# Regrouping the last six inverse-transform groups of the first batch with GpSimd copies, so that they run in 128x128 tiles in place of 128x64

## The chip, the cores and the metric

The kernel runs on one core of one Trainium2 chip. The metric is device time in microseconds (us), the median of repeated runs. A core has a matrix engine (TensorE, PE in the profile; its weight loads are listed apart as PEld), a vector engine (VectorE, DVE), a scalar engine (ScalarE, ACT), GpSimd (POOL) and a queue engine (SyncE, SP). POOL and SP also issue DMAs. Each engine works through its own instructions in the order in which the program wrote them and waits for others only by semaphores.

## The reference

For each of 8 batches of 3008 rows and 256 channels, a real FFT along the rows is multiplied by a learned filter and transformed back; the 24064 resulting rows then go through two matrix products with a leaky ReLU between them.

```python
X = np.fft.rfft(x, axis=1)                       # x: (8, 3008, 256)
Y = X * (filt_r + 1j * filt_i)[None]             # filters: (1505, 256)
y = np.fft.irfft(Y, n=3008, axis=1).reshape(24064, 256)
h = y @ w_in                                     # (256, 2048)
out = np.maximum(0.01 * h, h) @ w_out            # (2048, 256)
```

## The kernel before

**The transform.** 3008 is split into N1 x N2 = 94 x 32, with n = 32*n1 + n2. Forward stage 1 contracts over n1 and stage 2 over n2; the filter is applied; inverse stage "sa" contracts over the second frequency index, and inverse stage "sb" contracts over the first and gives 94 rows for each n2. Between the stages the layout has to be turned so that the contracted index lies on the partitions. The channels come in two halves, `dt` = 0 and 1, of 128 each. One sb group handles four values of n2 (h = 0 to 7) for one half `dt`.

**Two ways to run it.** Batches 1 to 7 turn the layout by DMA. For them `s1_group`, `s2_group`, `sa_group` and `sb_group` run a group of four small matmuls each (an s1 or sb group is four matmuls of 128x128 weights with some 94 to 96 moving columns). Batch 0 comes first, when nothing else can run, and is written out by hand in the list `FIRST`; it turns the layout with 32x32 block transposes on DVE (steps `t1`, `t2`). The last `t2` writes its result to `big[0]`. Because a transpose step moves pairs of 16-bit values, the 128 channels of one n2 lie in `big[0]` in two interleaved sets of 64, each with a step of four elements (8 bytes). `sb_matmuls` therefore takes each n2 in two matmuls with 128x64 weights, one writing PSUM partitions 0 to 63 and one 64 to 127: eight matmuls for a group of four n2.

`big[0]` holds 8192 elements a partition: `dt` = 0 in its first half and `dt` = 1 in its second. `FIRST` runs all eight groups of `dt` = 0 (`sbp 0 h`) and the groups h = 0 and 1 of `dt` = 1. The other six, h = 2 to 7 of `dt` = 1, are not needed by the first row chunk; `late_sb` runs them later, at the times in `REST`, in the order h = 2, 4, 5, 3, 7, 6. `quad_copy` evicts each from PSUM to `yt`, the rows that the matrix products read. From the fourth row chunk on, `big[0]` is reused for operand sums.

**The row chunks.** 47 chunks of 512 rows go through `moe1` (16 steps with 128x512 moving operand, evicted in pairs by ACT with the leaky ReLU, L531) and then through the second product: plainly for the first three chunks (`plain`, L693), and for the later ones with a Strassen-like scheme of seven products (`products`, L601, with its sums on DVE at L567).

**The order of the work.** Every piece of work is put with `at(time, f)` on a heap, in planned time units of which a chunk has eight, and is emitted in order of that time. This sets only the order in each engine's queue; the engines run as fast as their semaphores allow. The s1 groups of batch 1 are planned at 0.6-unit steps from the start; `x_load(2, ...)` (POOL-issued, 192 KB each) for batch 2 is planned from 9.6 units; the first filter addition on POOL (`y`, L330) follows after 12.6.

**Lines named below.** L269 and L270: matmuls and eviction of an s1 group. L277: DMA transposes of batch 1 on. L315: matmuls of an s2 group, L321 to L327 its filter products on DVE. L330: the addition on POOL. L337 and L339: sa. L351: eviction in `quad_copy`. L362: matmuls of an sb group of batches 1 to 7. L445: `t2`. L453: matmuls of `sb_matmuls`. L207: `x_load`; L474: load of `w_out`. L721: sums of weights on DVE. L726 to L728: DVE copies of the filter to the lower and upper 64 partitions. PSUM tiles are `ph` (two banks each), `pf` and `po_ps`.

Of the kernel before, what the change touches and what calls it, by code (L numbers as in the profile page):

```python
# [11 lines left out]
P = 128  # L12
# [7 lines left out]
N1, N2 = 94, 32  # L20
NC = 24
Q = 32
# [56 lines left out]
def kernel(  # L79
# [9 lines left out]
    nc = tc.nc  # L89
# [24 lines left out]
    REST = (5.339, 14.69, 8.396, 11.015, 24.419, 20.72)  # L114
# [21 lines left out]
    i1_sb = cpool.tile([P, N2, NW], FP16, name="i1_sb")  # L136
# [7 lines left out]
    HALF = Q * D // 2  # L144
    big = [cpool.tile([P, Q * D + (HALF // 2 if i == 2 else 0)], FP16, name=f"big{i}") for i in range(3)]
# [21 lines left out]
    def bank(kind, n, w, hold=0.75):  # L167
        if kind == "ph":
            t = wide[turn[kind] % 2]
            turn[kind] += 1  # L170
        else:
            i = min(range(len(single)), key=lambda i: frees[i])
            t, frees[i] = single[i], max(frees[i], clock["now"]) + hold
        return t[:, : n * w].rearrange("p (n w) -> p n w", n=n)
# [5 lines left out]
    def at(time, f):  # L180
        clock["n"] += 1
        heapq.heappush(work, (time, clock["n"], f))


    issued = set()

    def need(*what):
        for w in what:
            assert w in issued, w
# [155 lines left out]
    def quad_copy(b, h, dt, ps, copy):  # L345

        start, v, a = (b * N + h * QT) % RING, ps.rearrange("p c a -> p a c"), 0
        while a < N1:
            to = (start + 4 * a) % RING
            n = min(N1 - a, (RING - to) // 4)  # L350
            copy(yt[:, dt, ds(to, 4 * n)].rearrange("p (a c) -> p a c", c=4), v[:, ds(a, n)])  # L351
            a += n
# [15 lines left out]
    act, dve = nc.scalar.copy, nc.vector.tensor_copy  # L368
# [78 lines left out]
    def sb_matmuls(ps, dt, h):  # L447
        assert ("i1t",) not in issued
        src = big[0][:].rearrange("p (h n e r t) -> p h n r t e", h=2, n=Q // 2, r=2, t=2)
        for j in range(4):  # L450
            n2 = 4 * h + j
            for t in range(2):
                nc.tensor.matmul(ps[64 * t : 64 * t + 64, j, :], src[:, dt, n2 // 2, n2 % 2, t, :],  # L453
                                 i1_sb[:, n2, :N1], start=True, stop=True)
# [6 lines left out]
    def sbe(dt, h, e):  # L461
        quad_copy(0, h, dt, held.pop(("sb", dt, h)), engine[e])

    def late_sb(dt, h, copy):
        ps = bank("pf", 4, NW)[:, :, :N1]
        sb_matmuls(ps, dt, h)
        quad_copy(0, h, dt, ps, copy)

    def load_x(half):
        x_load(1, half * N2 // 2, N2 // 2)  # L470
# [229 lines left out]
        return [lambda tj=tj, ct=ct: one(tj, ct) for tj in range(4) for ct in range(NCT)]  # L700

    groups, first_use = [], {}
    for g in range(10, 16):
        at(REST[g - 10], lambda g=g: late_sb(1, g - 8, (act, dve)[g < 12 and g % 2]))

    def plan(b, s1, s1_step, s2, s2_step, lag, sb, sb_step, xl, x_step):
        for g in range(16):
# [23 lines left out]
    for b in range(1, B):  # L731
        z = 47 * (b - 4) if b > 4 else 0
        p = PLANS[min(b, 4) - 1]
# [23 lines left out]
    while queue:  # L757
        time, n, stage, b, g, f = heapq.heappop(queue)
        t = max(time, last + GAP)
# [64 lines left out]
```

## Time and profile before

| what | value |
|---|---|
| runs | 742.13 us median of 3 (745.01, 740.62, 742.13) |
| profiled execution | 740.67 us, its span from first to last instruction 738.9 us |
| granted TensorE clock | 0.999 |
| PE busy | 731.1 us (99%), PEld 522.1 us (71%) |
| DVE, ACT, POOL busy | 509.1, 549.1, 167.8 us (69, 74, 23%) |

The profile shows one execution, so a sum over its rows is made against 740.67 us. Busy shares are averages over the whole span; the change concerns the stretch from about 33 to 80 us, and there the timeline of each engine has to be read. A line of the timeline gives start, duration, engine, line of the program, operation, output and input, the number of instructions merged into it, and in brackets the idle time before it with what ended it. The start of the next PE line tells how long a group of matmuls held the stream; the duration in the line includes the drain of the last one.

### The profile page before, as it was taken

The numbers are of one execution on the slowest core, as the hardware profiler recorded it, in microseconds if no ns is written. First come the engines' busy times: TensorE is split into PE (matmuls) and PEld (weight loads), VectorE is DVE, ScalarE is ACT, GpSimd is POOL, SyncE is SP. The second block draws the span as 40 slices with busy tenths as digits, with TensorE's granted clock in tenths as the row PEclk, the third lists the DMA queues.
The fourth block names the chain that finished last, engine by engine and source line by source line (L and its number), as shares of the span: only waits on it lengthen the run. The fifth ranks groups of instructions, "written<-read, shape, count | busy, mean of one in ns | idle before, by whom it ended". The sixth has DMA issues, their size and how long they took to land.

```text
span 738.9 us, 19530 instructions
## 1 busy us (share of the span) xinstructions
PE 731.1 (99%) x8129; PEld 522.1 (71%) x8129; DVE 509.1 (69%) x696; ACT 549.1 (74%) x763; POOL 167.8 (23%) x171
## 2 busy tenths in 40 slices
PE   8999999999999999999999999999999999999997
PEld 3666677777777777777777777777767777777776
DVE  7978557776677667676777667676767686465566
ACT  4775787887788778887688877888767777777762
POOL 5605411433122322212232323122031210000000
PEclk9999999999999999999999999999999999999999
DMA  9978779777855595556855577434853432112012
GB/s 205 229 109 169 189 152 180 163 176 162 193 134 119 142 195 143 130 144 120 190 130 136 124 155 172 115 91 109 151 171 94 120 106 91 58 55 66 29 45 72
DMA packets 128617, 98.44 MB, mean 133 GB/s; under 512 B 59296, under 2 KB 107296, under 8 KB 128336
## 3 DMA queue, kind: packets, MB, share of 16 engines
q1 hardware_dynamic: 112752, 79.30, 41.8%
q0 software_dynamic: 15056, 17.50, 15.6%
q8 instruction: 63, 1.03, 0.6%
q10 hardware_dynamic: 720, 0.39, 0.2%
q14 instruction: 26, 0.21, 0.1%
HBM read 45.97 MB, written 35.65 MB: 110 GB/s over the span
## 4 chain that ended last, share of the span: by engine, by line
PE 95%; DVE 1%; DMA 1%; SPq 1%; ACT 1%; POOL 0%; issue 0%; POOLq 0%; DVEq 0%
PE ph L528 42%; PE pf L601 18%; PE po_ps L601 18%; PE pf L362 2%; PE pf L269 2%; PE pf L337 2%; PE pf L315 2%; PE po_ps L384 2%; PE pf L693 1%; PE po_ps L693 1%; DMA p_b_g<-p_b_g 1%; SPq L277 1%; POOL y_b_g L330 0%; PE pf L436 0%; ACT yt L351 0%; PE ph L412 0%
## 5 line engine op out<-in xcount | busy, mean ns | idle before, releaser
L531 ACT ACTIVATE gt_c<-ph 128x1024 f16<-128x1024 f32 x376 | 385.1, 1024 | 133.1 <-PE ph L528 126.2
L528 PE MATMUL ph<-yt,w_in_sb 128*128 128x512 f16 x1504 | 447.3, 379 | 0.2 <-ACT yt L351 0.2
L601 PEld LDWEIGHTS <-gt_c 128*128 128x128 f16 x2800 | 201.8, 98 | 98.2 <-issue 1.6
L330 POOL TENSOR_TENSOR y_b_g<-p_b_g,p_b_g 128x512 f16<-128x512 f32 x84 | 118.2, 1409 | 422.0 <-DMA p_b_g<-p_b_g 287.0
L601 PEld LDWEIGHTS <-big 128*128 128x128 f16 x2128 | 151.4, 98 | 65.9
L528 PEld LDWEIGHTS <-w_in_sb 128*128 128x128 f16 x1504 | 117.7, 98 | 4.4 <-DVE yt L351 0.4
L324 DVE TENSOR_TENSOR p_b_g<-pf,fb_sb 128x512 f32<-128x512 f32 x78 | 53.7, 689 | 33.4 <-PE pf L315 20.2
L601 PE MATMUL po_ps<-wt_sb,gt_c 128*128 128x128 f16 x704 | 71.8, 219 | 0.0
L601 PE MATMUL pf<-wt_sb,gt_c 128*128 128x128 f16 x688 | 69.3, 219 | 0.0
L601 PE MATMUL pf<-wt_sb,big 128*128 128x128 f16 x704 | 68.7, 219 | 0.0
L601 PE MATMUL pf<-w_out_sb,gt_c 128*128 128x128 f16 x720 | 68.1, 219 | 0.0
L351 ACT CAST yt<-pf 128x376 f16<-128x376 f32 (+9 forms) x136 | 58.2, 441 | 12.2 <-PE pf L362 8.5
L601 PE MATMUL po_ps<-w_out_sb,gt_c 128*128 128x128 f16 x688 | 65.7, 219 | 0.0
L601 PE MATMUL po_ps<-wt_sb,big 128*128 128x128 f16 x688 | 65.5, 219 | 0.0
L567 DVE TENSOR_TENSOR big<-big,gt_c 128x2048 f16<-128x2048 f16 (+1 forms) x45 | 57.5, 1278 | 0.1
L327 DVE TENSOR_TENSOR p_b_g<-pf,fa_sb 128x512 f32<-128x512 f32 x84 | 57.2, 681 | 0.2
L567 DVE TENSOR_TENSOR big<-gt_c 128x2048 f16<-128x2048 f16 (+1 forms) x46 | 56.8, 1234 | 0.0
L567 DVE TENSOR_TENSOR big<-gt_c,big 128x2048 f16<-128x2048 f16 (+1 forms) x45 | 56.6, 1258 | 0.0
L567 DVE TENSOR_TENSOR gt_c<-gt_c 128x2048 f16<-128x2048 f16 x43 | 55.6, 1293 | 1.0
L339 ACT CAST big<-pf 128x512 f16<-128x512 f32 x84 | 49.0, 583 | 9.3 <-PE pf L337 7.4
L270 ACT CAST big<-pf 128x384 f16<-128x384 f32 x90 | 43.0, 479 | 10.9 <-PE pf L269 8.3
L362 PE MATMUL pf<-i_sb,big 128*128 128x94 f16 x448 | 37.0, 206 | 0.0
(98 smaller groups left out, 645.8 us busy)
## 6 DMA issues: line engine op xcount, KB each, us to landing
p_b_g<-p_b_g SPq DMA_DIRECT2D x156, 128.0 KB
out_dram<-ost_c_h SPq DMA_DIRECT2D x117, 128.0 KB
dz<-big SPq DMA_DIRECT2D x42, 256.0 KB
big<-dz SPq DMA_DIRECT2D x56, 192.0 KB
x_sb<-in_x_dram POOLq DMA_DIRECT2D x40, 192.0 KB, 4.2
x_sb<-in_x_dram POOLq DMA_DIRECT2D x2, 768.0 KB, 9.4
w_in_sb<-in_moe_w_in_dram POOLq DMA_DIRECT2D x1, 1024.0 KB, 13.6
w_out_sb<-in_moe_w_out_dram POOLq DMA_DIRECT2D x1, 1024.0 KB, 14.5
```

Source lines behind the costliest of these rows:

```text
L269: nc.tensor.matmul(ps[:, j, :], x_sb[:, 4 * h + j, ts(dt, P)], fwd1m[:, :NW], start=True, stop=True)
L270: copy(turn_in[:, :, dt, :, ds(4 * h, 4)], ps.rearrange("p n (q k) -> p k q n", q=4))
L324: nc.vector.tensor_tensor(p2[:], ps, fb, AL.mult)
L327: nc.vector.tensor_tensor(p1[:], ps, fa, AL.mult)
L330: ("y", b, g), lambda: nc.gpsimd.tensor_tensor(y1[:], p1[:], p3[:], AL.add)))
L339: nc.scalar.copy(st2[h % 3][:, ds(2 * (g % 2), 2), :], ps)
L351: copy(yt[:, dt, ds(to, 4 * n)].rearrange("p (a c) -> p a c", c=4), v[:, ds(a, n)])
L362: nc.tensor.matmul(ps[:, j, :], z2[h % 3][:, j, ts(dt, P)], i1_sb[:, 4 * h + j, :N1], start=True, stop=True)
L528: nc.tensor.matmul(ph[:, j, :], w_in_sb[:, dt, ts(ct, P)], yt[:, dt, ds(ci * CH % RING, CH)], start=(dt == 0), stop=(dt == NDT - 1))
L531: nc.scalar.activation(gts[ci][:, ds(2 * g, 2), :], ph, AF.Lrelu)
L567: nc.vector.tensor_tensor(*(v[:, ds(c0, n)] for v in (o, i0, i1)), op)
L601: nc.tensor.matmul(of[t], a()[:, c, ts(t, P)], w[:, c, :], start=(c == 0), stop=(c == NCH - 1))
```

## The change

Six copies on GpSimd, emitted right after the hand-written list (planned time 0.02, in the order h = 2, 4, 5, 3, 7, 6), read the `dt` = 1 half of `big[0]`, which has the 8-byte step, and write it in plain [n2][channel] order into `rest`, the first 3072 elements of `big[0]`. That place held `dt` = 0, whose groups have run by then. Each copy moves 128 partitions x 512 16-bit elements. `late_sb` then runs each n2 in one matmul with 128x128 weights out of `rest`, four for a group in place of eight. Its planned times, its PSUM banks and its evictions stay.

```diff
+    rest = big[0][:, : 24 * P].rearrange("p (n d) -> p n d", d=P)
+
+    def regroup(h):
+        src = big[0][:, HALF:].rearrange("p (n e x) -> p n x e", n=Q // 2, x=4)
+        nc.gpsimd.tensor_copy(rest[:, ts(h - 2, 4)].rearrange("p (n r) (t e) -> p n (r t) e", r=2, t=2), src[:, ts(h, 2)])
+        issued.add(("rest", h))
+
-    def late_sb(dt, h, copy):
+    def late_sb(h, copy):
         ps = bank("pf", 4, NW)[:, :, :N1]
-        sb_matmuls(ps, dt, h)
-        quad_copy(0, h, dt, ps, copy)
+        need(("rest", h))
+        for j in range(4):
+            nc.tensor.matmul(ps[:, j, :], rest[:, 4 * (h - 2) + j], i1_sb[:, 4 * h + j, :N1], start=True, stop=True)
+        quad_copy(0, h, 1, ps, copy)
...
     groups, first_use = [], {}
+    for h in (2, 4, 5, 3, 7, 6):
+        at(0.02, lambda h=h: regroup(h))
     for g in range(10, 16):
-        at(REST[g - 10], lambda g=g: late_sb(1, g - 8, (act, dve)[g < 12 and g % 2]))
+        at(REST[g - 10], lambda g=g: late_sb(g - 8, (act, dve)[g < 12 and g % 2]))
```

## The prediction

> **What bounds the kernel now.** I read the page first, for the bound:
>
> ```profile
> PE 731.1 (99%) x8129; PEld 522.1 (71%) x8129; DVE 509.1 (69%) x696; ACT 549.1 (74%) x763; POOL 167.8 (23%) x171
> PE 95%; DVE 1%; DMA 1%; SPq 1%; ACT 1%; POOL 0%; issue 0%; POOLq 0%; DVEq 0%
> ```
>
> PE is busy for 731.1 of 738.9 us, and 95% of the chain that ended last is PE. So PE time taken out of the middle should come off the end, unless the stage it is taken from waits for something else. Next, the groups by shape from 0 to 110 us, for the prices (busy us, mean ns):
>
> ```profile
> L453 PEld LDWEIGHTS <-big 128*64 128x64 f16 x128 | 4.6, 154 | 2.6 <-issue 1.6 <-DVE big L445 1.0
> L269 PEld LDWEIGHTS <-x_sb 128*128 128x128 f16 x128 | 8.6, 98 | 4.4
> L330 POOL TENSOR_TENSOR y_b_g<-p_b_g,p_b_g 128x512 f16<-128x512 f32 x12 | 15.1, 1269 | 35.8 <-DVE p_b_g L327 26.6 <-DMA p_b_g<-p_b_g 5.6 <-PE pf L315 2.9
> ```
>
> A 64-column load from the stepped layout takes 154 ns, a plain one of 128 columns 98. Then the PE timeline around the first and the last of the six late groups, where the starts count:
>
> ```profile
> 40.81 0.59 PE L528 MATMUL ph<-yt,w_in_sb 128*128 128x512 f16 x2
> 41.34 0.45 PE L453 MATMUL pf<-i_sb,big 128*64 128x94 f16 x8
> 41.71 0.34 PE L269 MATMUL pf<-small_sb,x_sb 128*128 128x96 f16 x4
> 41.89 1.03 PE L528 MATMUL ph<-yt,w_in_sb 128*128 128x512 f16 x4
> 42.76 0.33 PE L269 MATMUL po_ps<-small_sb,x_sb 128*128 128x96 f16 x4
> ...
> 79.43 0.49 PE L693 MATMUL po_ps<-w_out_sb,gt_c 128*128 128x256 f16 x3
> 79.85 0.45 PE L453 MATMUL pf<-i_sb,big 128*64 128x94 f16 x8
> 80.23 0.60 PE L528 MATMUL ph<-yt,w_in_sb 128*128 128x512 f16 x2
> ```
>
> Last, DVE from 33 to 47 us with the DMA share of two stretches, and one place later on where POOL and DVE meet:
>
> ```profile
> 37.40 0.96 DVE L726 TENSOR_SCALAR fb_sb<-fa_sb 64x3072 f16<-64x3072 f16 x1
> 40.19 0.95 DVE L727 COPY fb_sb<-fa_sb 64x3072 f16<-64x3072 f16 x1
> 42.09 0.56 DVE L270 CAST big<-pf 128x384 f16<-128x384 f32 x1 [0.50 <-PE pf L269]
> 43.62 0.56 DVE L270 CAST big<-po_ps 128x384 f16<-128x384 f32 x1 [0.97 <-ACT gt_c L531]
> 44.21 0.95 DVE L728 COPY fa_sb<-fa_sb 64x3072 f16<-64x3072 f16 x1
> 45.19 1.02 DVE L270 CAST big<-pf 128x384 f16<-128x384 f32 x2
> ```
>
> ```profile
> 40.00:45.00 5.00, 5.00 (x52) 2.95 (x51) 3.50 (x6) 4.76 (x8) 0.00 (x0) 1.00 0.84 136
> 45.00:50.00 5.00, 4.93 (x46) 3.42 (x45) 3.26 (x7) 3.77 (x5) 0.00 (x0) 1.00 0.01 2
> ```
>
> ```profile
> 159.61 1.28 POOL L330 TENSOR_TENSOR y_b_g<-p_b_g,p_b_g 128x512 f16<-128x512 f32 x1 [5.20 <-DVE p_b_g L324]
> 160.03 1.94 DVE L567 TENSOR_TENSOR gt_c<-gt_c 128x2048 f16<-128x2048 f16 x1
> ```
>
> **What is removed: 24 of 48 small matmuls.** Four L528 go from 41.89 to 42.76, so a pair holds the stream 0.43 us; the pair at 40.81 was done at 41.24. The late group starts at 41.34, after a hole of 0.10, and the next work at 41.71: 0.47 us in all. At 79.43 three L693 (0.11 each: four go from 45.23 to 45.67) end at 79.76, and the next L528 starts at 80.23: 0.47 again; the groups at 51.58, 58.69 and 71.77 give the same. The new form, four matmuls with plain 128x128 weights and 94 columns, is almost the L269 group: 41.71 to 41.89, 0.17 to 0.18 us, with no hole ahead. So 0.47 - 0.17 = 0.30 us a group, 1.8 us for six.
>
> [...] Eight 64-column matmuls take 41.34 to 41.71, 46 ns each; four 128-column ones take 43 ns each. The two halves of an n2 do not run side by side. [...]
>
> **What of it reaches the end.** The first two late groups stand where ACT and DVE hold the chain: it runs L528 at 42.06, ACT L531 at 42.53, then DVE L270, L728 and L270 until 46.21, then the L269 at 46.27 that needed a bank. ACT had idled 0.23 us for PE before 42.53, so of the first 0.30 only 0.23 passes on. The group at 45.76 lies ahead of the L269 that waits for DVE, with a hole of 0.13 behind it already: its saving turns into a longer hole, so I count 0. The other four stand in a stream of PE work without such a hole: 4 x 0.30 = 1.2. After 110 us PE waits for another engine only twice, both for L330, 1.3 us in all, and these waits hang on filter products that PE itself released, so they move with it. Sum: 0.23 + 0 + 1.2 = 1.4 us.
>
> **What is added: six copies on POOL.** They need the last `t2` (DVE, ends 33.67) and, for h = 7, the last `dt` = 0 group (PE, before 34.5). The trace has no one-input copy on POOL and none with an 8-byte step. Nearest rows: L330, two 32-bit inputs of the same 512 elements, 1.27 us; L416, one 32-bit and one 16-bit input, 1.16 us mean. One input should be less; bounds 0.6 (half of 1.27) to 2.4 us (the longest L330 in this trace, 2.36, while it met DVE). I take 1.0, near L416. [...]
>
> Six copies and two meetings with DVE (L726, L727, 0.96 each) end at 33.67 + 6.0 + 1.9 = 41.6 us. The first is done by 34.7, needed at 41.34; the second by 35.7, needed at 45.76; the others are needed at 51.58, 58.69, 71.77 and 79.85. PE does not wait unless one copy takes over 6 us. The cover on POOL is its idle time: it issues the `w_out` load at 28.38, two `x_load`s of batch 2 at 36.46 and 37.67, and then nothing until L330 at 57.24. The two loads are queued behind the copies and move to about 41.6 and 42.2, landing by about 49 to 50 (7.4 us from issue). Their rows are first read at 82.08. They leave a full stretch of DMA (share 0.84) for an empty one (0.01), and end about where the first DMA transpose is issued (48.87): no charge. Were the copies 2.4 us each, these loads would run beside the transposes that the L315 at 54.57 waits for.
>
> **What is added on DVE: meetings with POOL.** Evictions from PSUM beside L330 keep their time (L324 and L327 at 57.13 and 57.73, inside an L330, took 0.69 and 0.68). L567, with both inputs in SBUF, took 1.94 instead of 1.22 us at 160.03: the 0.72 extra is about the rest of the L330 that ended at 160.89. The trace shows no L726-like one-input copy beside POOL. Bounds: nothing, or a full copy (1.0) for each of L726 and L727. I take half a copy each, 1.0 us by 41 us, at no cost: DVE idles 0.50 before 42.09 and 0.97 before 43.62, and a PSUM bank comes round only four groups later (the eviction that ends at 38.94 frees the bank used at 40.64). Without that cover up to 0.5 us would pass on.
>
> [...]
>
> **Sum.** 740.67 - 1.4 = 739.3 us for the profiled execution. That one lay 1.46 under the median of the runs; against the median, 742.13 - 1.4 = 740.7 us. Half a per cent, 3.7 us, is about what a measurement of this kernel can tell from no change, so this counts as none.
>
> **Rivals.**
> *The copies are slow, and DVE pays.* If a copy takes c, copies are still running when L728 starts at 44.21 as soon as 33.67 + 1.92 + 6c passes that, c > 1.44. What is left, 6c - 8.62, alternates with L728, L726 (47.23) and L721 (from 49.87), all SBUF to SBUF. DVE's idle time there is 0.42 + 1.23 + 1.26 = 2.9 us (before 46.64, 49.41 and 55.06), and the saving is 1.2. Net loss: 6c - 12.7, zero at c = 2.1, 1.7 us at 2.4 (743.8), 3.7 at 2.74. For: the unseen 8-byte step and first use of this operation. Against: two 32-bit inputs take 1.27.
> *The saving is absorbed.* The split tiles cost what whole ones do, or the later stages wait for SP's transposes and filter copies (chain: SPq 1%, DMA 1%) whatever PE does: 742.1. Against: 0.47 beside 0.17.
> *The saving passes on whole and takes stalls with it.* 1.8, the holes at 46.27 (0.13) and 70.81 (0.24), and the 1.3 of waits for L330: 3.5 us, 738.7. For: these waits sit at the edge. Against: they follow PE's own releases.
>
> **How the numbers follow.** Forecast 0.55, absorbed 0.12, whole and more 0.16, slow copies 0.17. Range: from the third rival, 738.7, to the slow copies at 2.4 us, 743.8. Faster by over 3.7 us needs the third rival and a little of the scatter of the runs (the lowest was 1.5 under the median): 0.13. Slower by over 3.7 needs c above 2.74, or a shift in the batch's SP queue that I don't see: 0.14. Within: 0.73.
>
> **What would show it.** The late groups as x4 with 0.17 us to the next start; six copies on POOL from 33.7, each about 1 us, ending near 42; L726 and L727 longer by up to a copy, L728 at 0.95; `x_load` at about 42; PE at the end of the last late group 1.4 us earlier than before. Copies over 2 us, or L728 stretched, would make the forecast wrong; so would a PE wait at a late group.

## The result and the profile after

| comparison | before, median | after, median | ratio (95% interval) |
|---|---|---|---|
| first | 741.58 us (6 runs) | 738.87 us (6 runs) | 0.9958 (0.9939 to 0.9977) |
| second (`e1_after_again`) | 740.93 us (31 runs) | 739.24 us (12 runs) | 0.9979 (0.9968 to 0.9990) |

The change makes the kernel faster. The first comparison says 0.42%, 3.1 us with an interval of 1.7 to 4.6; the forecast was 1.4 us, below it. (The ratio is not that of the two medians, which lie 2.7 us apart.) The second, with more runs, says 0.21%, 1.6 us (0.7 to 2.4), and holds the forecast. The six runs of before in the first comparison include one of 745.01 us; none of the 69 later runs of that kernel is above 743.0. Without it the means of the first comparison differ by 2.5 us instead of 3.1. The profiled execution took 738.81 us against 740.67, spans 737.0 and 738.9. First the page after: PE lost 1.3 us of busy time and is still the bound.

```profile
PE 729.8 (99%) x8105; PEld 521.4 (71%) x8105; DVE 511.1 (69%) x696; ACT 549.1 (75%) x763; POOL 171.1 (23%) x177
PE 95%; DVE 2%; ACT 1%; DMA 1%; SPq 1%; issue 0%; POOL 0%; DVEq 0%; ACTq 0%; POOLq 0%
```

The groups by shape from 0 to 110 us (busy us, mean ns). Line 475 is the late group's matmul, 468 the copy; later lines of the program have moved down by nine to eleven, so 528 is now 537, 693 is 702 and 726 to 728 are 737 to 739.

```profile
L475 PEld LDWEIGHTS <-big 128*128 128x128 f16 x24 | 1.7, 98 | 0.5
L468 POOL COPY big<-big 128x512 f16<-128x512 f16 x6 | 3.6, 648 | 4.3 <-DVE big L445 4.3
```

The weight loads take 98 ns, and a copy 0.65 us. The PE timeline around the first, the second and the last late group:

```profile
40.77 0.59 PE L537 MATMUL ph<-yt,w_in_sb 128*128 128x512 f16 x2
41.20 0.33 PE L475 MATMUL pf<-i_sb,big 128*128 128x94 f16 x4
41.36 0.34 PE L269 MATMUL pf<-small_sb,x_sb 128*128 128x96 f16 x4
...
45.31 0.33 PE L475 MATMUL pf<-i_sb,big 128*128 128x94 f16 x4
45.91 0.33 PE L269 MATMUL pf<-small_sb,x_sb 128*128 128x96 f16 x4 [0.27 <-DVE big L270]
...
78.15 0.49 PE L702 MATMUL po_ps<-w_out_sb,gt_c 128*128 128x256 f16 x3
78.48 0.33 PE L475 MATMUL pf<-i_sb,big 128*128 128x94 f16 x4
78.64 0.60 PE L537 MATMUL ph<-yt,w_in_sb 128*128 128x512 f16 x2
```

A group now holds the stream for 0.16 us, from 41.20 to 41.36, and starts the moment the pair ahead is through: the hole of 0.10 is gone. The second group's saving became a hole of 0.27 behind it, while the L269 waits for DVE. In the kernel before the same place read:

```profile
45.76 0.44 PE L453 MATMUL pf<-i_sb,big 128*64 128x94 f16 x8
46.27 0.33 PE L269 MATMUL pf<-small_sb,x_sb 128*128 128x96 f16 x4
46.44 0.59 PE L528 MATMUL ph<-yt,w_in_sb 128*128 128x512 f16 x2
```

POOL and DVE at the copies:

```profile
33.77 3.60 POOL L468 COPY big<-big 128x512 f16<-128x512 f16 x6 [4.29 <-DVE big L445]
37.33 1.59 POOL L207 DMA_DIRECT2D x_sb<-in_x_dram  x2
```

```profile
37.35 0.96 DVE L737 TENSOR_SCALAR fb_sb<-fa_sb 64x3072 f16<-64x3072 f16 x1
40.14 0.94 DVE L738 COPY fb_sb<-fa_sb 64x3072 f16<-64x3072 f16 x1
41.73 0.56 DVE L270 CAST big<-pf 128x384 f16<-128x384 f32 x1 [0.18 <-PE pf L269]
43.26 0.56 DVE L270 CAST big<-po_ps 128x384 f16<-128x384 f32 x1 [0.97 <-ACT gt_c L540]
43.85 0.95 DVE L739 COPY fa_sb<-fa_sb 64x3072 f16<-64x3072 f16 x1
44.83 1.02 DVE L270 CAST big<-pf 128x384 f16<-128x384 f32 x2
```

The six copies are over at 37.37, just as the first DVE filter copy starts at 37.35; it keeps its 0.96 us, so no meeting costs anything. The `x_load`s slip by under a microsecond. Last, two stretches by window; the last two columns are the DMA share and GB/s, and they show still a full stretch and an empty one.

```profile
40.00:45.00 5.00, 5.00 (x51) 3.08 (x50) 3.79 (x7) 4.99 (x8) 0.00 (x0) 1.00 0.81 132
45.00:50.00 5.00, 4.73 (x43) 3.34 (x41) 3.29 (x6) 3.41 (x5) 0.00 (x0) 1.00 0.04 8
```

**Where the time went.** I follow one `moe1` matmul after another through both timelines. At the start of the late groups the changed kernel is 0.04 us ahead (40.77 against 40.81), after the first 0.36 (41.53 for 41.89), after the second still 0.36 (46.08 for 46.44), after the sixth 1.59 (78.64 for 80.23), and from 82 us on 1.50 (80.86 for 82.36), because right behind the last group PE has two short holes, together 0.09, that it did not have before. That leaves 1.46 us from the late groups; the forecast was 1.43. Then the lead melts to 0.55 (536.21 for 536.76), a net loss of 0.95 in small stalls of 0.2 to 0.4 us between 100 and 270 us, and rises to 1.90 (537.24 for 539.14) at one place, where PE before waits long for L330 and PE after does not:

```profile
537.20 0.33 PE L601 MATMUL po_ps<-w_out_sb,gt_c 128*128 128x128 f16 x3
538.71 0.38 PE L337 MATMUL pf<-y_b_g,small_sb 128*128 128x512 f16 x1 [1.18 <-POOL y_b_g L330]
```

```profile
536.64 0.33 PE L610 MATMUL po_ps<-w_out_sb,gt_c 128*128 128x128 f16 x3
536.80 0.38 PE L337 MATMUL pf<-y_b_g,small_sb 128*128 128x512 f16 x1
```

### The profile page after: what moved, and what is told of

It is laid out like the page before. It is cut to its first block, busy times and chain, and to the rows that moved or that the text cites. A ratio compares the mean times of both kernels' runs of the same rounds, so it can differ in the third digit from the quotient of the medians.

```text
span 737.0 us, 19490 instructions
## 1 busy us (share of the span) xinstructions
PE 729.8 (99%) x8105; PEld 521.4 (71%) x8105; DVE 511.1 (69%) x696; ACT 549.1 (75%) x763; POOL 171.1 (23%) x177
## 4 chain that ended last, share of the span: by engine, by line
PE 95%; DVE 2%; ACT 1%; DMA 1%; SPq 1%; issue 0%; POOL 0%; DVEq 0%; ACTq 0%; POOLq 0%
PE ph L537 43%; PE po_ps L610 18%; PE pf L610 18%; PE pf L362 3%; PE pf L337 2%; PE pf L315 2%; PE pf L269 2%; PE po_ps L384 2%; PE pf L702 1%; PE po_ps L702 1%; DMA big<-big 1%; PE pf L436 0%; ACT yt L351 0%; PE ph L412 0%; DVE big L295 0%
## 5 line engine op out<-in xcount | busy, mean ns | idle before, releaser
L330 POOL TENSOR_TENSOR y_b_g<-p_b_g,p_b_g 128x512 f16<-128x512 f32 x84 | 117.8, 1403 | 420.9 <-DMA p_b_g<-p_b_g 288.7
L351 ACT CAST yt<-pf 128x376 f16<-128x376 f32 (+9 forms) x136 | 58.2, 441 | 12.0 <-PE pf L362 8.6
L576 DVE TENSOR_TENSOR gt_c<-gt_c 128x2048 f16<-128x2048 f16 x43 | 57.6, 1339 | 1.0
L576 DVE TENSOR_TENSOR big<-gt_c 128x2048 f16<-128x2048 f16 (+1 forms) x46 | 58.0, 1262 | 0.0
L576 DVE TENSOR_TENSOR big<-big,gt_c 128x2048 f16<-128x2048 f16 (+1 forms) x45 | 56.9, 1265 | 0.1
L576 DVE TENSOR_TENSOR big<-gt_c,big 128x2048 f16<-128x2048 f16 (+1 forms) x45 | 56.0, 1245 | 0.0
```

The lines of the kernel that those rows point to most:

```text
L330: ("y", b, g), lambda: nc.gpsimd.tensor_tensor(y1[:], p1[:], p3[:], AL.add)))
L576: nc.vector.tensor_tensor(*(v[:, ds(c0, n)] for v in (o, i0, i1)), op)
```

## The experiments

**The changed kernel again** (`e1_after_again`, no edit).

> The changed kernel once more, in five rounds, for its size. Theory A (the saving is PE time alone: 1.5 us by 81 us, and what the medians show beyond it is the chance of later waits for DMA): 1.5 us faster, ratio 0.998, with later waits of either sign in the trace. Theory B (the copies push the two x_loads back by about 1 us and so calm a stretch of DMA, which is worth another us or so): 2.7 us faster again, ratio 0.9963.

Measured: 0.9979 (0.9968 to 0.9990), 1.6 us. Theory A. Its profile has the lead of the late groups (0.28 us at the start of the row chunks, 1.76 at 81 us) and again no long wait at 536 us.

**The copies alone** (`e2_copies_only`).

```diff
         need(("rest", h))
-        for j in range(4):
-            nc.tensor.matmul(ps[:, j, :], rest[...], ...)
+        sb_matmuls(ps, 1, h)
```

> The six copies run as in the changed kernel, but the late groups read the stepped half as before, in eight 128x64 matmuls. It holds the cost of the copies and of the two x_loads behind them alone. Theory A: same time as before within 0.5 us (ratio 1.000), late groups 0.47 us each. Theory B: 1.2 us faster, ratio 0.9984. The rival of the slow copies would give a loss here.

Measured: 1.0001 (0.9993 to 1.0010). Copies and delayed loads are free within 0.7 us, and bring nothing: theory B falls.

**The matmuls alone** (`e3_no_copies`): the six `regroup` calls are left out.

> Four 128x128 matmuls a late group as in the changed kernel, but without the six copies (this leaves the regrouping out: they read the dt = 0 half as the last transpose left it). It holds the matmul saving alone. Theory A: as the changed kernel, 1.5 us faster, ratio 0.998, and 1.5 us ahead of before at 81 us. Theory B: 1.5 us faster where the changed kernel is 2.7 us faster.

Measured: 0.9978 (0.9967 to 0.9988), as the changed kernel. At 81 us it is 1.31 us ahead after a start 0.13 behind: 1.44 from the late groups. The whole gain is in the matmuls.

**Narrow tiles from plain order** (`e4_plain64`).

```diff
-            nc.tensor.matmul(ps[:, j, :], rest[:, 4 * (h - 2) + j], ...)
+            for t in range(2):
+                nc.tensor.matmul(ps[64 * t : 64 * t + 64, j, :], rest[:, 4 * (h - 2) + j, 64 * t : 64 * t + 64], ...)
```

> The copies run, and the late groups read the plain layout, but in eight 128x64 matmuls: only the number and width of the tiles is as before, the 8-byte step of the weights is gone. If the tile count and the switch of tile width make the cost: 0.47 us a group with the hole of 0.10 ahead, weight loads still longer than 98 ns, time as before. If the step makes it: weight loads of 98 ns or less, no hole, 8 x 0.04 = 0.32 us or less a group, half or more of the saving kept (0.9 us).

Measured: 1.0002 (0.9992 to 1.0011), so at most 0.6 us faster; in its timeline the late groups gain 0.44 us (from 0.27 behind the kernel before to 0.17 ahead at 80 us). The weight loads of its late groups, and its PE timeline at the last one:

```profile
L476 PEld LDWEIGHTS <-big 128*64 128x64 f16 x48 | 1.3, 113 | 1.6 <-issue 1.4 <-POOL y_b_g L330 0.2
```

```profile
79.35 0.49 PE L704 MATMUL po_ps<-w_out_sb,gt_c 128*128 128x256 f16 x3
79.77 0.36 PE L476 MATMUL pf<-i_sb,big 128*64 128x94 f16 x8
80.06 0.60 PE L539 MATMUL ph<-yt,w_in_sb 128*128 128x512 f16 x2
```

The hole is there (the three L704 end at 79.68, the group starts at 79.77), and the group then takes 0.29 in place of 0.37. Without the 8-byte step a group costs 0.38 of the 0.47 us. So the step makes 0.08, the narrow tiles 0.22: neither expectation alone, but mostly the first.

**Whole tiles with the step** (`e7_stepped128`): no copies, 128 columns with the 8-byte step taken straight from `big[0]`.

> No copies; four 128x128 matmuls a late group read their weights straight from big[0] with the 8-byte step (this mixes two n2 in one tile, so the late groups' numbers are left out; the cost is that of the step at full width). If the tile width makes the cost, 0.17 us a group and no hole, loads of 98 ns; if the step is as dear as in the narrow tiles (154 ns against 113 in plain order), 4 loads of some 140 ns or more and about 0.25 us a group.

Measured in one profile: loads of 113 ns (98 in plain order), and a group from 78.44 to 78.61, 0.17 us, no hole.

```profile
L475 PEld LDWEIGHTS <-big 128*128 128x128 f16 x24 | 1.8, 113 | 0.4
```

At full width the step costs the stream nothing. A version without copies would need the channels of one n2 to lie in one step, which the pairing of the 32-bit transpose prevents; the next experiment moves that into the transpose.

**The order made by the transpose** (`e6_layout`).

```diff
     def sae(hf, c, e):
...
-                  held.pop(("sa", hf, c)).rearrange("p n (t e) -> p n e t", t=2))
+                  held.pop(("sa", hf, c)).rearrange("p n (e t) -> p n e t", t=2))
     def t2(i):
-        o = ....rearrange("p (h n e r) -> p h e n r", ...)
+        o = ....rearrange("p (h n r e) -> p h e n r", ...)
     def sb_matmuls(ps, dt, h):
...
+            nc.tensor.matmul(ps[:, j, :], src[:, dt, n2], i1_sb[:, n2, :N1], start=True, stop=True)
```

> No copies: the last transpose itself writes [n2][channel] order (4-byte instead of 8-byte pieces on its output, and the eviction ahead of it pairs neighbouring channels), and all sixteen groups of the stage, the ten of the hand-written part too, run in 128x128 tiles. If the transposes keep their 1.2 us: 1.5 us from the six late groups as in the changed kernel, and 0.2 to 0.3 more from the first group ahead of the first eviction, the other early groups being behind ACT's evictions: 1.8 us faster, ratio 0.9976. If 4-byte pieces slow the transposes, each 0.1 us costs up to 0.4 in all; at 1.7 us each the gain is gone.

Measured: 1.0037 (1.0025 to 1.0049), 2.7 us slower. The late groups do save their time, but the transposes write 4-byte pieces and take 1.92 us each in place of 1.22 (mean in the kernel before):

```profile
L445 DVE STREAM_TRANSPOSE big<-big 128x1024 f32<-128x1024 f32 x4 | 7.3, 1920 | 0.0
```

PE waits for them twice, 1.26 and 1.53 us, and a second cost follows that I had not put down. The windows by stage (PE, PEld, DVE, ACT, POOL, then the granted PE clock, the DMA share and GB/s):

```profile
36.00:38.00 2.00, 1.51 (x15) 0.94 (x16) 1.02 (x3) 0.47 (x1) 0.00 (x0) 0.78 1.36 192
38.00:40.00 2.00, 2.00 (x11) 0.90 (x9) 1.12 (x2) 0.93 (x1) 0.41 (x1) 0.50 1.46 199
40.00:42.00 2.00, 2.00 (x19) 1.24 (x18) 1.46 (x2) 1.08 (x3) 0.67 (x2) 0.87 1.37 195
```

After the two waits the clock is at half for some 3 us while PE has work, and the kernel falls from 1.84 to 3.79 us behind between its first and fifth `moe1` pair. Eleven of the twelve runs of this kernel show a mean granted clock of 0.994 to 0.997, where the kernel before shows 0.999 to 1.0; the twelfth, with 0.999, is the fastest (741.29 us). Here the change's choice, whole tiles by a copy on an idle engine, is better than whole tiles by a dearer step on the path.

**Longer copying** (`e5_copies_x3`): twelve more copies behind the six.

```diff
-    for h in (2, 4, 5, 3, 7, 6):
+    for h in (2, 4, 5, 3, 7, 6) + (7, 6) * 6:
```

> The changed kernel with twelve copies more behind the six (h = 7 and 6 six times over again, the same result), so that the copies last long enough to meet the three DVE filter copies at 37.4, 40.2 and 43.9 us. Exclusive lock (a SBUF-to-SBUF DVE copy and a POOL copy shut each other out): each of the three DVE copies stretched by up to 0.6 us, each POOL copy that meets one stretched by 0.96; copies end at about 33.7 + 18 x 0.6 + 2.9 = 47.4; DVE's slack covers it, PE as in the changed kernel, ratio 0.998. No lock: all durations stay at 0.60 and 0.96, copies end at 44.5. The rival in which slow copies let DVE pay: from 6 x c = 10.8 it would be 1.9 us better than its break-even of 12.7, so still no loss; a loss here would mean its slack was over-counted.

Measured: 0.9981 (0.9972 to 0.9990), as the changed kernel. DVE and POOL in its timelines:

```profile
37.02 1.45 DVE L737 TENSOR_SCALAR fb_sb<-fa_sb 64x3072 f16<-64x3072 f16 x1
39.91 1.07 DVE L738 COPY fb_sb<-fa_sb 64x3072 f16<-64x3072 f16 x1
43.52 1.15 DVE L739 COPY fa_sb<-fa_sb 64x3072 f16<-64x3072 f16 x1
```

```profile
33.46 12.89 POOL L468 COPY big<-big 128x512 f16<-128x512 f16 x18 [3.54 <-DVE big L445]
```

All three DVE copies are stretched, by 0.5, 0.1 and 0.2 us. Three POOL copies, the ones that start while such a DVE copy runs, take 1.38 to 1.39 us; the others take 0.63 to 0.66:

```profile
L468 POOL COPY big<-big x18: 632/646/1392, 33.5 to 45.7; 128x512 f16<-128x512 f16 x18
```

At each meeting an instruction takes longer by about what is left of the other engine's running one, less some 0.1 us. The L567 at 160.03 in the kernel before shows the same beside L330: 1.94 us for 1.22, 0.72 longer, with 0.86 of the L330 left. So the expectation's second case, in which all durations stay, is out; its first gave POOL 0.96 more a meeting, and 0.73 to 0.75 was measured. The trace has one semaphore wait for the 18 copies, at 33.3 us ahead of the first: here two engines hold each other up without one. PE pays only at 45.78, where the L269 waits 0.47 for DVE instead of 0.27: 0.2 us, out of the meeting at L739, the one that stands on the chain.

**More of the old work** (`e9_late_twice`): the kernel before with `sb_matmuls(ps, dt, h)` written twice in `late_sb`.

> The kernel before with the eight 128x64 matmuls of each late group issued twice (same result): more of the same PE work in the same place. Theory A (PE time of these groups passes on one to one where PE has no hole): eight more at 46 ns are 0.37 us a group, 2.2 us for six, of which the group at 45.8 can hide 0.13; 2.1 us slower, ratio 1.0028. If such a stage had slack that the rest of the pipeline takes up, or gave more than one to one, it would be near 1.000 or above 1.005.

Measured: 1.0005 (0.9995 to 1.0014), 0.4 us slower: a miss. Its last group:

```profile
81.58 0.69 PE L453 MATMUL pf<-i_sb,big 128*64 128x94 f16 x16
82.20 0.61 PE L529 MATMUL ph<-yt,w_in_sb 128*128 128x512 f16 x2
```

Sixteen take 0.62 where eight took 0.37, so eight more cost 0.25 (31 ns each), not 0.37. From 0.61 behind ahead of the late groups it is 1.97 behind after them: 1.36 us of added delay. The runs show 0.4 (-0.4 to 1.0) of it; in its profile another 0.5 is lost between 150 and 250 us, and the wait at 536 us is gone and gives 1.3 back.

**What a narrow tile costs** (`e13_plain64_twice`, `e14_plain64_sides`, `e15_whole_twice`): the plain narrow tiles issued twice, the same once but all lower halves ahead of all upper ones, and the whole tiles twice.

> The plain 64-column tiles with each group's eight matmuls issued twice (same result). Theory S (halves of the two sides run side by side at full speed; the cost is a fixed 0.10 us at the entry and some 0.12 at the exit of the narrow tiles): 16 in 0.29 + 0.17 = 0.46 us. Theory N (each matmul costs its own 36 ns, side by side or not): 16 in 0.58 us.

> The plain 64-column tiles, but the four matmuls of the lower 64 PSUM partitions first and then the four of the upper (same result). Theory S: no neighbour on the other side to run with, so 8 x 0.042 + 0.12 = 0.46 us from the start of the group to the next start, against 0.29. Theory N: order does not matter, 0.29 us.

> The changed kernel with the four whole tiles of each late group issued twice (same result). Both theories: 43 ns for one more, 8 in 0.33 us, no hole and no fixed part.

Measured, one profile each, in this order:

```profile
41.30 0.52 PE L476 MATMUL pf<-i_sb,big 128*64 128x94 f16 x16
41.76 0.34 PE L269 MATMUL pf<-small_sb,x_sb 128*128 128x96 f16 x4
```

```profile
41.19 0.37 PE L476 MATMUL pf<-i_sb,big 128*64 128x94 f16 x8
41.49 0.34 PE L269 MATMUL pf<-small_sb,x_sb 128*128 128x96 f16 x4
```

```profile
41.45 0.50 PE L475 MATMUL pf<-i_sb,big 128*128 128x94 f16 x8
41.78 0.34 PE L269 MATMUL pf<-small_sb,x_sb 128*128 128x96 f16 x4
```

Sixteen plain halves take 0.46: eight more cost 0.17, 21 ns each, 42 for a pair, and a whole tile more costs (0.33 - 0.16) / 4, also 42. Theory S has that number. But the order by sides takes 0.30, not 0.46, so running next to a half of the other side is not what makes halves cheap in a way that order could spoil. What is shown: a pair of plain halves costs what a whole tile costs, and a group of narrow tiles pays 0.10 us ahead of it and 0.12 that does not grow with its size. No run shows what makes the 0.12. The weight loads show the 0.10 ahead. In the kernel before the first load of a narrow group starts with the group itself, after 0.42 us without a load; in the changed kernel the first load of a whole tile starts at 40.98, 0.22 us ahead of its matmul:

```profile
41.33 0.32 PEld L453 LDWEIGHTS <-big 128*64 128x64 f16 x8 [0.42 <-issue]
```

The two halves of a pair do overlap: in the kernel before they start within 0.01 us of each other, where the second whole tile of the changed kernel starts 0.04 us after the first. In `e14_plain64_sides` neighbours of the same side start 0.01 us apart too. How halves overlap stays open.

**The wait at 536 us** (`e8_before_again`, `e10_plain64_look`, `e11_copies_only_look`, `e12_no_copies_look`: one more profile each).

> The kernel before, profiled once more, to see whether its one long wait (PE for L330 at about 536 us, 1.2 us, absent from the profile of the changed kernel) belongs to the kernel or to the execution. If it belongs to the execution (DMA landing times), it can be absent here; if to the kernel, it is there again.

> Plain 64-column tiles, profiled once more for the long wait of PE for L330 at about 536 us. If the wait goes with the kernel's timing, it is absent again (as in the first profile of this kernel); if it goes with the execution, it may be there.

> Copies alone, profiled once more for the same wait: there again (1.2 us) if it goes with the kernel's timing, perhaps absent if it goes with the execution.

> Whole tiles without the copies (the regrouping is left out), profiled once more for the same wait: absent again if it goes with the kernel's timing, perhaps there if it goes with the execution.

Measured: 1.2 us again in the kernel before and with the copies alone; absent again with plain narrow tiles and with whole tiles without copies. So all four profiles in which the late groups cost what they did before have it, and one of the other thirteen, `e14_plain64_sides`, although its late groups cost the same as those of `e4_plain64`, which lacks it. It goes mostly with the kernel's timing, not with that alone.

The chain behind the wait in the kernel before tells more. It runs through SP's queue, where three DMA transposes come ahead, then through a DMA copy of the products that takes 4.06 us to land, and then through L330, which meets L567 on DVE:

```profile
530.53 1.34 SPq L277
531.99 0.53 SPq L325
532.57 4.06 DMA p_b_g<-p_b_g
536.78 1.88 POOL y_b_g L330
```

```profile
536.32 1.22 DVE L567 TENSOR_TENSOR big<-big,gt_c 128x2048 f16<-128x2048 f16 x1
```

In the changed kernel SP issues the same copy at 531.83, 0.74 us earlier, where PE is 0.55 ahead: so far it moves with PE. But it has landed by 534.40, at most 2.6 us from issue, and L330 starts ahead of that L567 (now L576):

```profile
534.40 2.03 POOL L330 TENSOR_TENSOR y_b_g<-p_b_g,p_b_g 128x512 f16<-128x512 f32 x1 [6.97 <-PE ph L537]
535.76 1.76 DVE L576 TENSOR_TENSOR big<-big,gt_c 128x2048 f16<-128x2048 f16 x1
```

This order sorts all seventeen profiles. In the five with the wait, L330 starts 0.1 to 0.6 us after that DVE sum and takes 1.8 to 2.3 us; in the twelve without, it starts ahead of it, by 0.03 to 1.5 us. It also tells `e14_plain64_sides` from `e4_plain64`: in the first L330 starts 0.44 us after the sum and takes 1.89 us, in the second 0.09 ahead of it and takes 1.27. What sets how long the copy takes to land stays open. The runs without a profile can't show the wait, so that it makes the difference between 1.5 and 2.7 us is not shown.

## Why the prediction was right or wrong

**Right: the local sum.** 0.30 us a group was measured as 0.31; the first group passed on 0.32 (forecast 0.23), the second 0, the other four 0.31, 0.31, 0.32 and 0.29. That is 1.55, of which 0.09 is lost right behind the last group; 1.46 is left, for 1.43. So the agreement to 0.03 is partly luck: two misses of 0.1 cancel. The first group passed on more than ACT's idle 0.23 because ACT's eviction of that group (L351) moved too, from 41.83 to 41.72. PE never waited for a copy, as said, and copies alone cost nothing (1.0001). The `x_load`s came at 37.3 and not at 41.6, and the 1.0 us of meetings on DVE did not come, since the copies were shorter.

**Right in kind, wrong in size: the copy.** 0.65 us, not 1.0; the lower bound of 0.6 was near. So no copy met DVE. No run shows the two waits of 0.96 us that the prediction put into the end of the copies; in `e5_copies_x3` a copy that met a DVE copy took 0.73 to 0.75 longer. The rival of the slow copies was priced with a break-even at six copies of 2.1 us, 12.7 us of copying; with 12.9 us of copying in `e5_copies_x3` PE lost only 0.2. That the two engines hold each other up is real (1.38 us there for 0.65, and DVE copies longer by 0.1 to 0.5); with copies of 0.65 us its price to PE was one meeting's remainder, 0.2 us, not the whole of the time that copies go on. Single copies of 2 us, as that rival has them, were not run.

**Wrong: what becomes of it behind.** The step that failed is the sentence that the waits of PE for L330 after 110 us "hang on filter products that PE itself released, so they move with it", by which the later waits stood in the sum as nothing. The long one, 1.18 us at 538.7, did not move but vanished, and a net 0.95 us of other small stalls came: +0.4 us in all, and the profiled execution is 1.9 us shorter in span where 1.4 was forecast. What this wait hangs on is a DMA copy of 4.06 us that took at most 2.6 after the change, and which of L330 and L567 starts first. In the six profiles with whole tiles issued once, the lead over the kernel before changed by -0.5 to +1.1 us between 82 us and the end. So the later waits should have been a term of about plus or minus 1 us. The third rival had counted on this wait, and the profiled execution is between the forecast and it.

The rest of the first comparison's 3.1 us stands in no trace. 0.6 of it is the one run of 745.01 us, and the excess did not come again: three later comparisons of kernels with whole late tiles, `e1_after_again`, `e3_no_copies` and `e5_copies_x3`, give 0.9979, 0.9978 and 0.9981, that is 1.6, 1.6 and 1.4 us. They agree with the 1.4 of the sum. Why the first comparison came out larger stays open beyond that.

**Wrong: "so this counts as none".** The prediction took 3.7 us as about what a measurement of this kernel can tell from no change. The half-width of the first interval is 1.4 us and that of the second 0.8, and each of the four comparisons tells the change from none. A saving of 1.4 us should have been forecast as faster.

**Wrong in its reading, without effect on the sum: "the two halves of an n2 do not run side by side".** 46 ns each was 0.37 us divided by eight, and a third of that, 0.12, is a fixed part of the group. One more stepped half costs 31 ns, one more plain half 21, so a pair of plain halves costs what one whole tile does, 42 ns. The saving of 0.30 is 0.10 for the hole, 0.12 for the fixed part and 0.08 for the step; it is not that twice the matmuls take twice the time.

## What to carry to other kernels

A group's cost divided by its number of instructions is a mean, not a price: run it twice, and the difference is the price of one more, the rest a fixed part (here eight more stepped halves cost 0.25 us, where the first eight took 0.37). Where PE is the bound, time taken from its stream at 40 to 80 us shows as a shift of the starts behind it, and that shift can be read to 0.05 us from two timelines, where six runs of each kernel were good to about 1.4. Whether the shift lasts to the end depends on later waits, and one that hangs on a DMA landing need not move with PE (here 4.06 us from issue to landing before, at most 2.6 after). In this kernel an idle engine that puts data into the order that the bound engine reads best is a good trade as long as its meetings with DVE end before DVE's work stands on the chain (the one meeting that did not, at L739 in `e5_copies_x3`, cost PE 0.2 us).

## What was not expected of the hardware

- A POOL copy of 128x512 16-bit elements with an 8-byte step on its input took 0.65 us, half of the 1.27 of the addition with two 32-bit inputs.
- A DVE 32x32 transpose of 128x1024 32-bit elements took 1.22 us when it wrote 8-byte pieces and 1.92 when it wrote 4-byte pieces.
- After PE waits of 1.26 and 1.53 us within some 5 us, the granted clock fell to 0.50 for about 3 us, and the kernel fell another 1.9 us behind.
- The 8-byte step cost a weight load of 128 columns 15 ns (113 against 98) and the stream nothing; it cost 64-column loads 41 ns (154 against 113) and the stream 10 ns a matmul.
